# Layer 2 of a two-layer network by seven products: block sums of W2 kept in DRAM, and a fixed order of steps

## The chip, the cores and the metric

The kernel runs on one core of one Trainium2 chip. Its engines are TensorE (PE in the profile, its weight loads PEld), VectorE (DVE), ScalarE (ACT), GpSimd (POOL) and SyncE (SP), which issues most DMAs. The metric is the device time of one execution in microseconds (us).

## What is computed

```python
# q, k, v: (8, 8, 576, 64)
k_p = k.reshape(B, H, 72, 8, D).mean(axis=3)
v_p = v.reshape(B, H, 72, 8, D).mean(axis=3)
attn = softmax(q @ k_p.T / sqrt(D))            # 576 x 72 for each batch and head
x = (attn @ v_p) as (8, 576, 512)
xn = (x - mean(x)) / sqrt(var(x) + 1e-6) * g_ln
out = x + relu(xn @ w_ch1) @ w_ch2             # w_ch1: 512 x 2048, w_ch2: 2048 x 512
```

So there are 8 x 576 = 4608 tokens of 512 features. A small pooled attention makes x; then a network of two layers, the large part of the work, is added to it.

## The kernel before

**Chunks and tiles.** The tokens are cut into nine chunks of 512 (`CH`), each of four tiles of 128 (`TPC`). For a tile t, `stage_a` makes the attention scores and probabilities (`scores`, L495; `probs`, L523), and `stage_b` the values, the statistics of the normalisation and the normalised rows z (`values`, L612). For a chunk there is layer 1 (`ffn_in`, or from chunk 2 on `ffn_seven`) and layer 2 (`ffn_out`, L870).

**Precision by parts.** A product of two float32 matrices is made of float16 parts: each operand is a high part (rounded) plus a low part (the rest), and three matmuls, high x high, high x low and low x high, add up in PSUM. So each operand needs a pass that rounds (on ACT) and a pass that subtracts (on DVE or GpSimd). `split`, `parts_t` and `split_t` do this for weights, z and block sums.

**Seven products.** From chunk 2 on, layer 1 is made by Strassen's scheme in Winograd's form. Each operand is cut into 2 x 2 blocks, and seven block products take the place of eight. The right factors of W1 are the blocks B11, B21, B22 and the sums T1 to T4 (`sums_w`, `sum_last`, kept in SBUF), the left ones the blocks A11, A12, A22 of z and the sums S1 to S4, which `values` makes for the last two tiles of a chunk. `FACTOR` pairs them. `product` (L807) makes one of the seven for one block f of 128 hidden features: 6 matmuls of 128 x 128 weights on 256 columns. Products 1 and 6 and 7, 5 and 3, and 2 then 4 share a PSUM bank, so a bank is read out between two of them: `first_products`, `middle_products` and `last_product` copy the results out on ACT or add them on DVE, in a float32 buffer `cc`. Then, for each half of the tokens, ACT makes the ReLU's high part (L857) and DVE the low part (L858), into a `ring` tile.

**Layer 2** is made in the plain way: for a tile tt and a half of the hidden features, 24 matmuls of 512 columns (L882) add up in one PSUM bank, and one DVE instruction (L893) scales the sum by the token's factor and adds it to x. After the second half the rows are stored to `out`.

**Other work in the same queues.** GpSimd makes the pooled K and V of each of the eight batches (`pool_k` L368, `pool_v` L381) from loads on SP (`load_k`, `load_v`; two buffers each), the low part of the probabilities (L537) and those of z (L753). DMA transposes on SP turn probabilities and z (`transpose_z`, L756). `token_scales` (L712) makes 1/sqrt by three Newton steps on four numbers per partition, on DVE.

**Order.** Engines run their queues in program order. Chunks 0 and 1 and what belongs to them follow `START`, a list of steps written out by hand: a token such as `A.8` names a generator, here `stage_a(8)`, and each time it stands in the list the generator runs on to its next `yield`. From chunk 2 on a loop (L992) writes the order: per chunk 4 steps of `ffn_seven` and 4 of `ffn_out` for each half of the hidden features, with the next chunk's stages put between at the places `A_AT` and `B_AT`, and all the K and V work of a batch in one go.

**Memory.** PSUM has eight banks: two for scores and values (`ps_a`), six (`ps_g`) for the products. `ring` has two tiles for the hidden layer, `t_raw` two buffers for `cc`, `phl` two for the probabilities.

Of the kernel before, what the change touches and what calls it, by code (L numbers as in the profile page):

```python
# [104 lines left out]
def attn_ffn_kernel(ctx: ExitStack, tc: tile.TileContext, qT, kT, v, kvn, kvt, g, w1, w2, out):  # L105
# [506 lines left out]
    def values(t):  # L612
# [66 lines left out]
        if seven:  # L679
            yield  # L680
        (nc.gpsimd if c < 2 else nc.vector).tensor_scalar(
            out=z, in0=x, scalar1=ln[:, 0:1], scalar2=ln[:, 2:3], op0=ALU.subtract, op1=ALU.mult
        )
# [5 lines left out]
        elif tt < 2:  # L689
# [4 lines left out]
            yield from parts_t(z, 0, NKT, zTs[c][:, :, tt * P : (tt + 1) * P])  # L694
        else:
            zr, was = t_raw["z"], Z[t - 2]
            za = zr[:, 5 * HC : 7 * HC]
            nc.vector.tensor_scalar(
                out=za, in0=X[t - 2], scalar1=was[:, 0:1], scalar2=was[:, 2:3], op0=ALU.subtract, op1=ALU.mult
            )  # L700
# [104 lines left out]
    PS, C7 = {}, {}  # L805

    def product(c, h, f, m, start, stop):  # L807

        if start and m != 4:
            PS[f, m] = psum["ps_f"].tile([P, CH], F32, name="ps_f")  # L810
        ps = PS[f, {6: 1, 7: 1, 3: 5, 4: 2}.get(m, m)][:, :HC]
# [35 lines left out]
    def last_product(c, h, f):  # L847
        cc = C7.pop(f)
        u3 = product(c, h, f, 7, False, True)
        for j in range(2):  # L850
            nc.vector.tensor_tensor(out=cc[:, j, HC:], in0=u3, in1=cc[:, j, HC:], op=ALU.add)  # L851
# [188 lines left out]
```

## Time and profile before

| | us |
|---|---|
| median of three runs (lowest, highest) | 842.06 (841.86, 843.77) |
| the profiled execution | 842.33 |
| its span, first to last instruction | 840.6 |
| PE busy | 809.4 |
| DVE busy | 545.3 |
| POOL busy | 347.0 |
| ACT busy | 339.1 |

The profile is of one execution. Its span is what the instructions cover; the execution's own time is 1.7 us more. A line such as L882 is that line of the kernel. A group of instructions has one line, engine, operation and shape; it gives the count, the busy time (overlaps counted once), the mean length of one in ns, and the idle time of the engine ahead of them with what ended it. Matmuls overlap in the pipeline, so their mean length is more than their spacing. Of the span, the first 243 us hold the loading and splitting of the weights and chunks 0 and 1; chunks 2 to 8 fill the rest.

### The profile page before, as it was taken

The numbers are of one execution on the slowest core, as the hardware profiler recorded it, in microseconds if no ns is written. First come the engines' busy times: TensorE is split into PE (matmuls) and PEld (weight loads), VectorE is DVE, ScalarE is ACT, GpSimd is POOL, SyncE is SP. The second block draws the span as 40 slices with busy tenths as digits, with TensorE's granted clock in tenths as the row PEclk, the third lists the DMA queues.
The fourth block names the chain that finished last, engine by engine and source line by source line (L and its number), as shares of the span: only waits on it lengthen the run. The fifth ranks groups of instructions, "written<-read, shape, count | busy, mean of one in ns | idle before, by whom it ended". The sixth has DMA issues, their size and how long they took to land.

```text
span 840.6 us, 14847 instructions
## 1 busy us (share of the span) xinstructions
PE 809.4 (96%) x5742; PEld 527.5 (63%) x5742; DVE 545.3 (65%) x1110; ACT 339.1 (40%) x636; POOL 347.0 (41%) x497
## 2 busy tenths in 40 slices
PE   6797999999989999998999998999999999999998
PEld 3776454444557675757585857584858485858483
DVE  5988997674767476746764686559555856484242
ACT  4879784231424342423251515242524252424040
POOL 1898989684777442444225162402110211020000
PEclk9999999999999999999999999999999999999999
DMA  9848565232564515552434143513241424130001
GB/s 362 310 156 237 203 151 134 67 74 61 124 180 83 122 43 126 110 121 54 121 69 120 43 134 75 116 39 94 78 88 39 101 51 76 27 101 14 1 1 51
DMA packets 145975, 87.37 MB, mean 104 GB/s; under 512 B 125424, under 2 KB 126576, under 8 KB 143728
## 3 DMA queue, kind: packets, MB, share of 16 engines
q1 hardware_dynamic: 144752, 85.52, 39.2%
q10 hardware_dynamic: 1152, 0.90, 0.5%
q8 instruction: 45, 0.74, 0.4%
q14 instruction: 26, 0.21, 0.1%
HBM read 45.09 MB, written 9.44 MB: 65 GB/s over the span
## 4 chain that ended last, share of the span: by engine, by line
PE 70%; DVE 10%; POOL 9%; DMA 4%; issue 3%; ACT 2%; ACTq 0%; SPq 0%; POOLq 0%; DVEq 0%
PE ps_f L882 34%; PE ps_f L817 25%; PE ps_f L784 5%; PE ps_a L501 3%; DMA vr<-in_v_dram 2%; POOL vr L385 2%; POOL vr L386 1%; DVE w L264 1%; POOL vp L387 1%; POOL kblk L375 1%; PE ps_m L441 1%; POOL pt L575 1%; PE ps_a L633 1%; DVE w L211 1%; PE ps_a L634 1%
## 5 line engine op out<-in xcount | busy, mean ns | idle before, releaser
L882 PE MATMUL ps_f<-w,ring 128*128 128x512 f16 x1728 | 380.7, 379 | 0.0
L882 PEld LDWEIGHTS <-ring 128*128 128x128 f16 x1728 | 167.7, 98 | 193.8 <-issue 0.2
L817 PE MATMUL ps_f<-zts,w 128*128 128x256 f16 x1680 | 209.0, 274 | 8.2 <-DVE rowmax L168 3.4
L817 PEld LDWEIGHTS <-w 128*128 128x128 f16 x1680 | 164.2, 98 | 30.1 <-issue 8.9
L893 DVE SCALAR_TENSOR_TENSOR x<-ps_f,cy,x 128x512 f32<-128x512 f32 x72 | 53.8, 748 | 114.4 <-PE ps_f L882 107.8
L537 POOL TENSOR_TENSOR phl<-e,phl 128x512 f16<-128x512 f32 x32 | 38.5, 1204 | 142.5 <-ACT phl L527 142.4
L817 PE MATMUL ps_f<-zts,tsp 128*128 128x256 f16 x672 | 96.1, 272 | 0.3 <-ACT raw L835 0.3
L784 PE MATMUL ps_f<-zts,w 128*128 128x512 f16 (+1 forms) x480 | 87.0, 340 | 3.2 <-DVE ring L795 2.4
L857 ACT ACTIVATE ring<-raw 128x512 f16<-128x512 f32 x112 | 64.8, 622 | 58.4 <-DVE raw L851 57.9
L858 DVE SCALAR_TENSOR_TENSOR ring<-raw,ring 128x512 f16<-128x512 f32 x112 | 81.6, 755 | 8.7 <-ACT ring L857 8.4
L835 ACT COPY raw<-ps_f 128x256 f32<-128x256 f32 x56 | 20.8, 371 | 138.2 <-PE ps_f L817 134.8
L753 POOL TENSOR_TENSOR hl<-raw,hl 128x640 f16<-128x640 f32 x28 | 41.4, 1495 | 81.4 <-ACT hl L751 45.6
L784 PEld LDWEIGHTS <-w 128*128 128x128 f16 x480 | 47.0, 99 | 40.0 <-issue 3.7
L817 PEld LDWEIGHTS <-tsp 128*128 128x128 f16 x672 | 64.0, 98 | 10.7 <-issue 0.5
L385 POOL TENSOR_TENSOR vr<-vr 72x256 f32<-72x256 f32 x56 | 50.0, 898 | 34.3 <-DMA vr<-in_v_dram 34.0
L851 DVE TENSOR_TENSOR raw<-ps_f,raw 128x256 f32<-128x256 f32 x112 | 42.3, 418 | 22.6 <-PE ps_f L817 22.6
L838 DVE TENSOR_TENSOR raw<-ps_f,raw 128x256 f32<-128x256 f32 x56 | 23.7, 424 | 48.4 <-PE ps_f L817 43.0
L844 DVE TENSOR_TENSOR raw<-ps_f,raw 128x256 f32<-128x256 f32 x56 | 23.5, 420 | 32.6 <-PE ps_f L817 27.4
L751 ACT CAST hl<-raw 128x640 f16<-128x640 f32 x28 | 19.2, 722 | 62.6 <-DVE a L728 26.3
L501 PE MATMUL ps_a<-kblk,q 128*128 128x144 f32 (+1 forms) x320 | 43.1, 288 | 0.9 <-DVE st L661 0.9
L501 PEld LDWEIGHTS ps_a<-kblk,q 128*128 128x128 f32 (+1 forms) x320 | 39.1, 179 | 6.4 <-issue 1.3
L753 POOL TENSOR_TENSOR hl<-z,hl 128x512 f16<-128x512 f32 x18 | 21.5, 1196 | 36.0 <-ACT hl L751 22.7
(144 smaller groups left out, 1002.9 us busy)
## 6 DMA issues: line engine op xcount, KB each, us to landing
q<-in_qT_dram SPq DMA_DIRECT2D x36, 256.0 KB
out_dram<-x SPq DMA_DIRECT2D x36, 256.0 KB
tsp<-in_w_dram SPq DMA_DIRECT2D x8, 1024.0 KB
kr<-in_kT_dram SPq DMA_DIRECT2D x28, 288.0 KB
vr<-in_v_dram SPq DMA_DIRECT2D x56, 144.0 KB
raw<-in_w_dram SPq DMA_DIRECT2D x6, 1024.0 KB
ring<-in_w_dram SPq DMA_DIRECT2D x2, 1024.0 KB
w<-in_kT_dram SPq DMA_DIRECT2D x2, 576.0 KB
```

What stands on the lines that cost most here:

```text
L385: eng.tensor_add(out=vr[:, 0:4, :], in0=vr[:, 0:4, :], in1=vr[:, 4:8, :])
L501: nc.tensor.matmul(ps[r, p // 2, p % 2 * 2 * KV : (p % 2 + 1) * 2 * KV], lhsT=q[:, p, r], rhs=kblk[b % NKB][:, p, :], start=True, stop=True,)
L537: nc.gpsimd.tensor_tensor(out=ph[:, 0, :, KA:P], in0=e[:, :, 0:KA], in1=ph[:, 0, :, 0:KA], op=ALU.subtract)
L753: nc.gpsimd.tensor_tensor(out=zhl[:, 1, :], in0=src, in1=zhl[:, 0, :], op=ALU.subtract)
L784: nc.tensor.matmul(ps, lhsT=w[:, part, fs], rhs=zT[:, kz, cols], start=(n == 0), stop=(n == 3 * NKT - 1),)
L817: nc.tensor.matmul(ps, lhsT=w[:, part, f * P : (f + 1) * P], rhs=z, start=start and n == 0, stop=stop and n == 3 * KH - 1, skip_group_chec ...
L838: nc.vector.tensor_tensor(out=cc[:, 0, :HC], in0=m2, in1=cc[:, 0, :HC], op=ALU.add)
L851: nc.vector.tensor_tensor(out=cc[:, j, HC:], in0=u3, in1=cc[:, j, HC:], op=ALU.add)
L857: nc.scalar.activation(out=hh[:, 0, f], in_=cc[:, j], func=AF.Relu)
L858: nc.vector.scalar_tensor_tensor(out=hh[:, 1, f], in0=cc[:, j], scalar=0.0, in1=hh[:, 0, f], op0=ALU.max, op1=ALU.subtract)
L882: nc.tensor.matmul(ps, lhsT=h[:, part, i, cols], rhs=w[:, wp, j], start=(n == 0), stop=(n == 3 * NFT // 2 - 1),)
L893: nc.vector.scalar_tensor_tensor(out=x, in0=ps, scalar=out_scale(c, tt, half), in1=x, op0=ALU.mult, op1=ALU.add)
```

## The change

**Layer 2 of chunks 3 to 8 by seven products.** `out_seven(c, h, n, u)` makes product n of half h for 128 rows u: 12 matmuls on 256 columns, into three PSUM banks per u. After each product one DVE instruction scales what is in the bank and adds it to a 256-column half of x, or, for the last product, to both halves at once. `ffn_out` remains for chunks 0 to 2.

**The left factors** come from the hidden layer. `left_factors` makes the ReLU of the left half and splits A11 and A12, `right_relu` that of the right half and splits A22, `right_sums` makes S1 to S4 by four float32 sums of 256 elements on GpSimd, and `right_pair` splits them, two at a time: rounding on ACT, subtracting on DVE for S1 and S2, on GpSimd for S3 and S4. They lie where W2 was.

**The right factors** are W2's blocks and block sums. `keep_w2` stores B11, B21, B22 to a DRAM tile, `sums_w2` makes T1 to T4 (16 steps, during chunk 2 and the start of chunk 3) and stores them too. `load_w2` brings one factor of one half, 128 x 4096 bytes, back into one of four buffers in `ring`, 14 loads per chunk.

**Smaller edits.** From chunk 3 on z is normalised on ACT instead of DVE; product 7's two additions become one DVE instruction with the PSUM operand read twice; one of the two buffers of probabilities becomes the third `cc` buffer; `token_scales` is cut into steps. `first_products`, `middle_products`, `last_product` and `ffn_seven` are dissolved: each of the seven products and each later pass is a step of its own (`P`, `WH`, `EL`, `ER`, `ES`, `EP`, `O`, ...).

**A fixed order.** A list `STEADY` of 3398 tokens, built as `START` is, takes the place of the loop for chunks 2 to 8. All steps named above stand in it one by one, as do the single loads of W2, K and V and the single transposes.

```diff
+C_TWO = 3
-A_AT, B_AT = (0, 2, 5, 8), (4, 6, 11, 12)
+LO_GPSIMD = ()
+STEADY = """
+P.2.0.0.2 P.2.0.1.1 P.2.0.1.2 P.2.0.0.1 TW.0.0.0 TW.0.0.1 P.2.0.1.1 P.2.0.1.1 P.2.0.0.1 P.2.0.0.1 TW.0.0.0 TW.0.0.1
...
+O.5.1.1.1 O.5.1.1.1 O.5.1.0.0 O.5.1.0.0 O.5.1.1.0 O.5.1.1.0 B.27 B.27 ES.5.1.3 O.5.1.2.1 O.5.1.2.0 O.5.1.2.1 O.5.1.2.1
...
+O.8.1.5.1
+"""
...
-        ph = phl[t % 2]
+        ph = phl[t % 2 if t < 3 * TPC else 0]
...
+    def product(c, h, f, m):
+        if m in (1, 2, 5):
+            PS[c, h, f, m] = psum["ps_f"].tile([P, CH], F32, name="ps_f")
+        ps = PS[c, h, f, {6: 1, 7: 1, 3: 5, 4: 2}.get(m, m)][:, :HC]
...
+        yield
+        cc = left_buffer(c, h, f)
+        j, k = divmod({1: 0, 2: 0, 3: 2, 4: 1, 5: 3, 6: 2, 7: 1}[m], 2)
+        o = cc[:, j, k * HC : (k + 1) * HC]
+        if m in (2, 3):
+            nc.vector.tensor_tensor(out=o, in0=ps, in1=o, op=ALU.add)
+        elif m == 7:
+            o = cc[:, :, HC:]
+            nc.vector.tensor_tensor(out=o, in0=ps.unsqueeze(1).broadcast_to([P, 2, HC]), in1=o, op=ALU.add)
+        else:
+            nc.scalar.copy(out=o, in_=ps)
...
+    def split_h(src, n, f, engine):
+        hi, lo = (wt[2][:, n, a, f * HC : (f + 1) * HC] for a in range(2))
+        nc.scalar.copy(out=hi, in_=src)
+        yield
+        engine.tensor_tensor(out=lo, in0=src, in1=hi, op=ALU.subtract)
+
+    def left_factors(c, h, f):
+        cc = left_buffer(c, h, f)[:, :, :HC]
+        nc.scalar.activation(out=cc, in_=cc, func=AF.Relu)
+        yield from split_h(cc, slice(0, 2), f, nc.vector)
+
+    def right_relu(c, h, f):
+        cc = left_buffer(c, h, f)
+        nc.scalar.activation(out=cc[:, :, HC:], in_=cc[:, :, HC:], func=AF.Relu)
+        yield from split_h(cc[:, 1:2, HC:], slice(2, 3), f, nc.vector)
...
+    def right_sums(c, h, f):
...
+        nc.gpsimd.tensor_tensor(out=s_tmp[:, 0], in0=r01, in1=r11, op=ALU.add)
+        nc.gpsimd.tensor_tensor(out=s_tmp[:, 1], in0=s_tmp[:, 0], in1=r00, op=ALU.subtract)
+        yield
+        nc.gpsimd.tensor_tensor(out=s_tmp[:, 3], in0=r10, in1=s_tmp[:, 1], op=ALU.subtract)
+        nc.gpsimd.tensor_tensor(out=s_tmp[:, 2], in0=r00, in1=r01, op=ALU.subtract)
+
+    def right_pair(c, h, f, i):
+        yield from split_h(s_tmp[:, 2 * i : 2 * i + 2], slice(3 + 2 * i, 5 + 2 * i), f, nc.gpsimd if i or c in LO_GPSIMD else nc.vector)
...
+    def sums_w2(h, f, e):
...
+        for i in range(2):
...
+            nc.vector.tensor_tensor(
+                out=b[:, 2 * i : 2 * i + 2], in0=src[:, 0, e::2], in1=src[:, 1, e::2], op=ALU.add
+            )
+        yield
+        b11, b12, b21, b22 = (b[:, i] for i in range(4))
+        nc.gpsimd.tensor_tensor(out=b11, in0=b12, in1=b11, op=ALU.subtract)
+        nc.gpsimd.tensor_tensor(out=b12, in0=b22, in1=b12, op=ALU.subtract)
+        yield
+        nc.gpsimd.tensor_tensor(out=b22, in0=b22, in1=b11, op=ALU.subtract)
+        nc.gpsimd.tensor_tensor(out=b21, in0=b21, in1=b22, op=ALU.subtract)
+        yield
+        nc.scalar.copy(out=t[:, :, 0], in_=b)
+        yield
+        nc.gpsimd.tensor_tensor(out=t[:, :, 1], in0=b, in1=t[:, :, 0], op=ALU.subtract)
...
+    W2_USE = (("A11", "B11"), ("A12", "B21"), ("A22", "T4"), ("S1", "T1"), ("S2", "T2"), ("S4", "B22"), ("S3", "T3"))
...
+    def load_w2(c, h, n):
+        nc.sync.dma_start(out=w2_buffer(c, h, n), in_=w2s[h][W2_AT[W2_USE[n][1]]])
...
+    def out_seven(c, h, n, u):
+        left, b = H_AT[W2_USE[n][0]], w2_buffer(c, h, n)
+        if n in (0, 1, 3):
+            PO[c, h, u, n] = psum["ps_f"].tile([P, CH], F32, name="ps_f")
+        ps = PO[c, h, u, {0: 0, 1: 1, 2: 1, 3: 3, 4: 0, 5: 3, 6: 0}[n]][:, :HC]
+        for f in range(FPQ):
+            for part, wp in ((0, 0), (0, 1), (1, 0)):
+                nc.tensor.matmul(
...
+        yield
...
+        nc.vector.scalar_tensor_tensor(out=x, in0=ps, scalar=scale, in1=x, op0=ALU.mult, op1=ALU.add)
...
-    for c in range(2, NRUN):
...
-            all_of(op(*args))
+    run(STEADY)
```

More of the change, by code (lines that the diff above doesn't have):

```diff
@@ L802, in ffn_in, with left_buffer @@
         )
[L805 to L811, printed above, removed]
+    PS, C_BUF = {}, []
+    def left_buffer(c, h, f):
+        if "c" not in t_raw:
+            t_raw["c"] = t_raw.pop("t1").rearrange("p n c -> p (n c)").rearrange(
+                "p (i f c) -> p i f c", i=2, f=2
+            )
+        if c < C_TWO:
+            return t_raw["c"][:, f % 2]
+        if not C_BUF:
+            raw = phl[1].rearrange("p a h k -> p (a h k)").bitcast(F32).rearrange("p (i c) -> p i c", c=CH)
+            C_BUF.extend((t_raw["c"][:, 0], t_raw["c"][:, 1], raw))
+        return C_BUF[(2 * FPQ * c + FPQ * h + f) % 3]
+    def product(c, h, f, m):
+        if m in (1, 2, 5):
+            PS[c, h, f, m] = psum["ps_f"].tile([P, CH], F32, name="ps_f")
+        ps = PS[c, h, f, {6: 1, 7: 1, 3: 5, 4: 2}.get(m, m)][:, :HC]
         lname, rname = FACTOR[m]
@@ new lines, in attn_ffn_kernel @@
+    PO = {}
+    def out_seven(c, h, n, u):
[6 more added lines that the diff above has]
+                nc.tensor.matmul(
+                    ps,
+                    lhsT=wt[2][:, left, part, f * HC + u * P : f * HC + (u + 1) * P],
+                    rhs=b[:, f // FPB, wp, f % FPB],
+                    start=n < 4 and f == 0 and part == wp == 0,
+                    stop=f == FPQ - 1 and part == 1,
+                    skip_group_check=True,
+                )
+        yield
+        tt = u + 2 * (n in (2, 3, 6))
+        t = c * TPC + tt
+        x, scale = X[t], out_scale(c, tt, h)
+        if n == 6:
+            x = x.rearrange("p (j c) -> p j c", j=2)
+            ps = ps.unsqueeze(1).broadcast_to([P, 2, HC])
+        else:
+            x = x[:, HC:] if n in (3, 4, 5) else x[:, :HC]
+        nc.vector.scalar_tensor_tensor(out=x, in0=ps, scalar=scale, in1=x, op0=ALU.mult, op1=ALU.add)
+        if h == 1 and n in (5, 6):
+            yield
+            nc.sync.dma_start(out=out[t * P : (t + 1) * P, :], in_=X.pop(t))
@@ L975, in all_of, with run @@
             pass
-    begun = {}
-    with tc.manual_schedule():
-        for token in START.split():
-            if token not in begun:
-                name, *args = token.split(".")
-                begun[token] = iter(ops[name](*map(int, args)) or ())
-            next(begun[token], None)
-        for steps in begun.values():
-            all_of(steps)
+    def run(tokens):
+        begun = {}
+        with tc.manual_schedule():
+            for token in tokens.split():
+                if token not in begun:
+                    name, *args = token.split(".")
+                    begun[token] = iter(ops[name](*map(int, args)) or ())
+                next(begun[token], None)
+            for steps in begun.values():
+                all_of(steps)
+    run(START)
     first.close()
```

412 lines of the change are left out of this document (345 added, 67 removed).

## The prediction

> **What bounds the kernel now.** I read the page first for the share of each engine, then the busy times of the seven seven-product chunks side by side, then the chain that ended last for the pace of a matmul, and last what TensorE waited for.
>
> ```profile
> span 840.6 us, 14847 instructions
> ...
> PE 809.4 (96%) x5742; PEld 527.5 (63%) x5742; DVE 545.3 (65%) x1110; ACT 339.1 (40%) x636; POOL 347.0 (41%) x497
> ```
>
> The whole run is TensorE's. By chunk, from the first product of chunk 2 (columns: start and end, length, busy time of PE, PEld, DVE, ACT, POOL, granted clock, DMA share, GB/s):
>
> ```profile
> 243.00:331.00 88.00, 85.82 (x633) 57.87 (x632) 54.13 (x123) 30.16 (x64) 44.33 (x79) 0.98 0.44 105
> 331.00:418.00 87.00, 84.37 (x628) 57.86 (x627) 54.78 (x122) 31.44 (x67) 36.43 (x60) 1.00 0.44 99
> 418.00:503.50 85.50, 85.50 (x652) 58.07 (x650) 55.83 (x118) 31.59 (x67) 31.89 (x51) 1.00 0.37 93
> 503.50:590.40 86.90, 84.58 (x627) 57.79 (x625) 56.13 (x123) 31.17 (x67) 23.34 (x37) 1.00 0.37 84
> 590.40:675.50 85.10, 85.10 (x651) 58.04 (x650) 52.34 (x113) 30.70 (x66) 15.39 (x18) 1.00 0.32 72
> 675.50:758.60 83.10, 83.10 (x618) 56.74 (x617) 51.56 (x111) 30.67 (x66) 13.95 (x14) 1.00 0.33 64
> 758.60:840.60 82.00, 78.28 (x529) 51.56 (x527) 29.58 (x57) 20.24 (x48) 0.00 (x0) 1.00 0.05 17
> ```
>
> TensorE idles 2.18, 2.63 and 2.32 us in chunks 2, 3 and 5, together 7.1 us, and 3.72 us at the end, where the last row block is scaled and stored. Nothing else has more than two thirds of a chunk. So in these 597.6 us time falls only if TensorE gets less to do, and rises if another engine gets more than TensorE has.
>
> **The pace of a matmul.** The groups by shape mislead here:
>
> ```profile
> L882 PE MATMUL ps_f<-w,ring 128*128 128x512 f16 x1728 | 380.7, 379 | 0.0
> L817 PE MATMUL ps_f<-zts,w 128*128 128x256 f16 x1680 | 209.0, 274 | 8.2 <-DVE rowmax L168 3.4 <-DVE x L893 1.8 <-DVE raw L838 1.5
> L817 PE MATMUL ps_f<-zts,tsp 128*128 128x256 f16 x672 | 96.1, 272 | 0.3 <-ACT raw L835 0.3
> ```
>
> Busy time over count gives 380.7/1728 = 220 ns for 512 columns and (209.0+96.1)/2352 = 130 ns for 256. But these groups alternate in short runs, and the pipeline's tail is counted at the end of each run. In the chain (start, length, what) a long run stands undisturbed:
>
> ```profile
> 132.69 15.54 PE ps_f L882 x72
> ...
> 758.76 16.38 PE ps_f L817 x150
> ```
>
> 15.54/72 = 215.8 ns for 512 columns, 16.38/150 = 109.2 ns for 256, each with its own weight load. Halving a matmul costs 1%, not 18%.
>
> **What goes, on TensorE.** Layer 2 of a chunk is 192 matmuls of 512 columns, 41.4 us. By seven products it is 2 halves x 7 products x 2 row blocks x 12 = 336 of 256 columns, 36.7 us. That is 4.74 us less per chunk, 28.5 us in six. Scores, values and layer 1 keep their matmuls. The profiled run took 842.33 us, 1.7 us more than its span and 0.3 us more than the median: 842.33 - 28.5 = 813.8 us if all idle time stays, 806.7 us if the 7.1 us go too. Busy time also counts the tail of the matmul ahead of a gap, 379 - 216 = 0.16 us by the rows above, so some idle time is hidden in it; for about 20 ends of runs I allow 3 us, and 803 us is the floor.
>
> The idle time, by what ended it:
>
> ```profile
> PE ps_f L817 <- DVE rowmax L168: 3.4, 2, 2.6
> PE ps_f L817 <- DVE x L893: 1.8, 2, 1.3
> PE ps_f L817 <- DVE raw L838: 1.5, 1, 1.5
> ```
>
> The 3.4 us are the maximum over V, whose small matmul stands in TensorE's order ahead of products that don't need it. The fixed order can put it, and the products that need late transposes, behind others, so I let these gaps go and charge what is new.
>
> **What comes, on DVE and ACT.** I build chunk 6 from its row (52.34 and 30.70 us) and these:
>
> ```profile
> L858 DVE SCALAR_TENSOR_TENSOR ring<-raw,ring 128x512 f16<-128x512 f32 x112 | 81.6, 755 | 8.7 <-ACT ring L857 8.4
> L857 ACT ACTIVATE ring<-raw 128x512 f16<-128x512 f32 x112 | 64.8, 622 | 58.4 <-DVE raw L851 57.9
> L893 DVE SCALAR_TENSOR_TENSOR x<-ps_f,cy,x 128x512 f32<-128x512 f32 x72 | 53.8, 748 | 114.4 <-PE ps_f L882 107.8
> L851 DVE TENSOR_TENSOR raw<-ps_f,raw 128x256 f32<-128x256 f32 x112 | 42.3, 418 | 22.6 <-PE ps_f L817 22.6
> ```
>
> DVE loses, per chunk, 16 of L858 (12.1 us) and the 8 evictions L893 (6.0), and its 16 adds L851 (6.7) become 8 of 512 elements (6.0). It gains 8 x (two low parts of 512 and one of 256) = 8 x 1.93 = 15.4, and 28 evictions of layer 2, 24 of 256 and 4 of 512, 13.0 us. That makes 62 us of about 80, less what the six normalisations moved to ACT give back. ACT loses 16 of L857 (10.0) and gains five passes of 512 and one of 256 (no dearer than 0.62) per block, 8 x 3.7 = 29.9, and six normalisations, 3.7: 54 us of 80. Both fit. What lies behind a late DVE instruction is an eviction, and behind that a product that adds onto the same bank (the first and the fifth, the second and the third). Two products of 1.3 us lie between most such pairs and an eviction takes 0.42, so I price this at 2.5 us, bounds 0 and 9 (a whole L893, 0.75 us, in each of the 12 halves). In chunk 2 the sums over W2 add 32 DVE passes of 256 (13.4 us on 54.1) and 16 ACT passes (10.0 on 30.2), which the 84 us there cover. The probabilities share one buffer from chunk 3 on; their tiles are some 20 us apart, so I cost that at nothing.
>
> **What comes, on GpSimd.** This is where the change can fail. Its prices, from chunk 2 on:
>
> ```profile
> L753 POOL TENSOR_TENSOR hl<-raw,hl 128x640 f16<-128x640 f32 x24 | 35.4, 1492 | 75.3 <-ACT hl L751 39.5 <-issue 35.9
> L537 POOL TENSOR_TENSOR phl<-e,phl 128x512 f16<-128x512 f32 x23 | 26.6, 1156 | 141.0 <-ACT phl L527 141.0
> L385 POOL TENSOR_TENSOR vr<-vr 72x256 f32<-72x256 f32 x29 | 23.3, 810 | 31.4 <-DMA vr<-in_v_dram 31.3
> L753 POOL TENSOR_TENSOR hl<-z,hl 128x512 f16<-128x512 f32 x12 | 14.6, 1218 | 28.0 <-ACT hl L751 14.8 <-DVE raw L698 8.5 <-issue 3.7
> L386 POOL TENSOR_TENSOR vr<-vr 72x128 f32<-72x128 f32 x30 | 13.9, 471 | 0.5
> L375 POOL TENSOR_TENSOR kblk<-kr 64x72 f32<-64x72 f32 x32 | 13.7, 427 | 4.0 <-PE ps_a L501 2.5
> L371 POOL TENSOR_TENSOR kr<-kr 128x288 f32<-128x288 f32 x14 | 11.5, 821 | 23.9 <-DMA kr<-in_kT_dram 23.8
> L387 POOL TENSOR_TENSOR vp<-vr 72x64 f32<-72x64 f32 x30 | 9.6, 330 | 4.5 <-DVE vb L211 2.5 <-DVE cvm L640 1.4
> L372 POOL TENSOR_TENSOR kr<-kr 128x144 f32<-128x144 f32 x14 | 7.2, 521 | 0.2
> L540 POOL TENSOR_TENSOR phl<-e,phl 128x64 f16<-128x64 f32 x23 | 7.0, 305 | 0.0
> L673 POOL COPY ln<-cv 128x2 f32<-128x2 f32 x18 | 5.6, 347 | 3.7 <-DVE cv L461 3.5
> ```
>
> Four sums of 256 elements go by L385 (0.81), a low part of 512 by L537 (1.16), W2's four sums of 128 by L386 (0.47). I count the fixed order from its start to the first V step of the last batch, well into chunk 4's last products. TensorE has there 170 products of layer 1 (111.3 us), the 8 row blocks of chunk 2 (41.4), 48 products of layer 2 (62.9) and 13 tiles of scores and 12 of values, some 1.5 us together for each (chunk 6's 85.1 less its 78.1 us of products, over five tiles), 19 us: 235 us. GpSimd has 64 sums (51.8), 16 low parts (18.5), all 16 W2 sums at 4 x 0.47 + 1.16 (48.6), 12 pairs of K at 0.82 + 0.52 + 2 x 0.43 (26.4), 31 heads of V at 0.81 + 0.47 + 0.33 (49.9), 13 probability splits (15.0), 12 z parts of 640 and 6 of 512 (25.2), 13 tails L540 and 12 copies L673 (8.1): 243 us, 8 more than TensorE. GpSimd, half idle so far, thus gets as much as TensorE for nearly three chunks, in a queue where each instruction waits for the one before. After that batch it falls to 51 us of 80: 15.39 + 8 x (4 x 0.81 + 1.16).
>
> These rows hold the collisions of today, and the change adds more. A DVE instruction with two SBUF inputs and a GpSimd one exclude each other (start, length, instruction):
>
> ```profile
> 319.78 0.15 DVE L729 TENSOR_TENSOR a<-a,ve 128x4 f32<-128x4 f32 x1
> 320.34 2.76 POOL L753 TENSOR_TENSOR hl<-raw,hl 128x640 f16<-128x640 f32 x2 [4.22 <-ACT hl L751]
> 320.36 1.40 DVE L729 TENSOR_TENSOR a<-a,ve 128x4 f32<-128x4 f32 x1
> ```
>
> The same four-element product took 0.15 us alone and 1.40 us when GpSimd had begun 0.02 us before: it waited for that whole instruction. The stretch has about 48 such DVE passes of 512 elements and 72 of 256; if each stopped GpSimd for half its 755 or 418 ns, that is 33 us; if none did more than today's, nothing. The Trainium skill, "SBUF — State Buffer", section "SBUF: two separate sides", calls it an exclusive lock held for a whole instruction and speaks against this change, which puts work on both sides of it; the trace agrees (1.40 against 0.15). By that rule, with every pass colliding, the sum would come to the top of the third case below.
>
> I take 9 us for GpSimd: the 8 of the sum and little of the collisions, since K and V may be late for a while and only S1 to S4 hold TensorE up. Bounds: 0, and the 41 of sum and collisions.
>
> **What moves, on the queues.** SP gains 14 loads of 0.5 MB per chunk, 7.3 MB in 80 us, about 92 GB/s on the 72 of chunk 6, with 38 stores in chunk 2, those of the second half's sums the last, a whole half before their use; a load waits until the product four places back is done, and K, V, Q loads and transposes stand behind it. Four products of two blocks last 10.5 us, so the loads are covered at four buffers; uncovered, the price is in the last case.
>
> Sum: 806.7 + 9 + 2.5 = 818 us.
>
> **The rivals.** *The order holds:* GpSimd's idle stretches in the order take up the excess, 803 to 808 us. For it: the rows' means hold waits, L385's 0.81 us and L753's 1.49 among them, so the bare instructions take less; against it: a GpSimd that is busy all the time meets DVE more often, not less. *GpSimd sets the pace:* the collisions are paid, 806.7 + 8 + half to all of 33 = 831 to 848 us; for it the 1.40 us row; against it, that a pass only collides when GpSimd is busy, and that L858 has a mean of 755 ns today beside a half-busy GpSimd. *Slower:* GpSimd's queue waits for K and V loads. Place: chunks 2 to 4, where an instruction that adds K or V rows stands ahead of the sums for S1 to S4 and its load has not landed. Price: the idle times in the rows L385 and L371, 31.3 + 23.8 = 55 us for the same loads, free so far since GpSimd was half idle. All of it on top of the 8 gives 870 us; it decides from 30 of the 55 on, since then GpSimd is 38 us late and 806.7 + 38 = 844.9 is the first time that counts as slower. Against it: the order puts each load well ahead of its use. *Not what it says:* 256-column products at 130 ns would make layer 2 43.7 us and gain nothing; the long run excludes it.
>
> **Chances.** Forecast, 808 to 831 us: 0.55. The order holds: 0.15. GpSimd sets the pace: 0.20. Loads hold GpSimd: 0.10. A measurement of this kernel can tell about 0.3% from no change, so faster means under 839.8 us: 0.55 + 0.15 + 0.13 of the third case = 0.83. Its part from there to 844.9 us has 0.05. Its top, 0.02, and the last case make slower 0.12. The range from the floor of 803 to 842 us leaves out those and half of the middle part.
>
> **What would show it.** In the changed profile: from chunk 3 on no matmul of 512 columns and 672 of 256 at 109.2 ns per chunk; POOL at nine tenths or more from 243 to about 480 us and some six tenths after; TensorE's new waits there behind the low parts of S1 to S4, at the fourth to seventh product of a half; the last two chunks without gaps, about 78 and 77 us. Wrong if the pace of 256 columns exceeds 112 ns, if the idle time lies in the last chunks, or if it ends on DVE's evictions or on W2's loads.

## The result and the profile after

The changed kernel takes 835.88 us (median of six runs, 834.55 to 839.23) beside 842.74 us of the kernel before on the same chip: a ratio of 0.9929, 95% interval 0.9902 to 0.9955. It is faster by 6.9 us. The forecast was 818 us: the direction was right and the range held, but the gain is little more than a quarter of the 24 us forecast.

Line numbers from here on are those of the changed kernel: L1134 the matmuls of `product`, L1251 those of `out_seven`, L1268 its VectorE eviction, L1170 the ScalarE cast and L1172 the subtraction that make a high and a low part (`split_h`; the subtraction is on VectorE or on GpSimd), L1189 to L1193 GpSimd's sums for S1 to S4, L1021 to L1023 the Newton steps behind the tokens' inverse roots, L1213 the first adds of W2's block sums. L1148 adds a product from PSUM to `cc` on VectorE, L1153 copies one on ScalarE, L1059 makes z's low parts on GpSimd, L1164 the low parts of the plain hidden layer, L1285 has the matmuls of the plain layer 2, and L442 the maximum over V. The page:

```profile
span 833.7 us, 17487 instructions
...
PE 787.5 (94%) x6606; PEld 609.8 (73%) x6606; DVE 671.7 (81%) x1242; ACT 472.5 (57%) x880; POOL 615.3 (74%) x817
```

DVE rose from 65% to 81% and POOL from 41% to 74%, while PE fell from 96% to 94%: TensorE got less to do and waits more. The steady part in stretches (start and end, length, busy time of PE, PEld, DVE, ACT, POOL, granted clock, DMA share, GB/s):

```profile
243.00:331.00 88.00, 82.25 (x645) 56.20 (x644) 79.57 (x142) 43.30 (x87) 76.79 (x122) 1.00 0.63 151
331.00:411.00 80.00, 76.59 (x683) 64.09 (x681) 68.69 (x130) 51.20 (x103) 76.20 (x107) 0.99 0.74 200
411.00:491.00 80.00, 76.81 (x750) 67.60 (x748) 71.19 (x133) 50.38 (x102) 68.43 (x94) 0.99 0.67 182
491.00:571.00 80.00, 76.87 (x736) 68.14 (x733) 67.35 (x132) 48.09 (x98) 60.39 (x84) 1.00 0.70 185
571.00:651.00 80.00, 76.80 (x756) 68.04 (x757) 68.34 (x128) 48.81 (x100) 55.40 (x72) 1.00 0.64 170
651.00:731.00 80.00, 78.08 (x756) 70.02 (x754) 65.16 (x130) 51.04 (x103) 48.63 (x56) 1.00 0.56 154
```

The idle time is in every stretch, also where POOL has fallen to 49 us of 80. DVE stands at 65 to 71 us of 80 throughout. What TensorE waits for (total, times, longest):

```profile
PE ps_f L1251 <- DVE w L1172: 7.2, 8, 1.7
PE ps_f L1251 <- DVE x L1268: 7.1, 8, 1.5
PE ps_f L464 <- DVE rowmax L442: 2.9, 1, 2.9
PE ps_f L1285 <- DVE ring L1164: 2.1, 4, 1.0
PE ps_f L1251 <- DVE phl L1148: 0.6, 1, 0.6
...
PE ps_f L1251 <- POOL w L1172: 0.2, 1, 0.2
```

All of the first five end on VectorE: on its low parts, on its evictions, on the maximum over V. On the low parts that GpSimd makes, TensorE waits only 0.2 us.

To compare runs I use two sums over each trace. *Idle time*: from the first product of the steady part on, what the distance between the starts of two matmuls exceeds the median of its kind by, where that is over 0.02 us; this also counts the gaps that busy time hides. *Waits* of an engine: what each of its instructions after 243 us took beyond the quickest twentieth of its kind. By the first, the 6.9 us of span come apart so: TensorE's own work after the first product (each matmul at the median of its kind) falls from 582.3 to 555.4 us, that product starts 2.2 us earlier, the idle time rises from 12.3 to 34.0 us, and the tail is 0.3 us longer; -26.9 - 2.2 + 21.7 + 0.3 = -7.1, which is the 6.9 within what the small distances leave out. The forecast had about 17 us of idle time. The second sum says where to look: VectorE's waits rose from 32 to 110 us, GpSimd's from 14 to 47, ScalarE's are 5. Some groups of VectorE (count, busy us, mean ns):

```profile
L1172 DVE TENSOR_TENSOR w<-raw,w 128x256 f16<-128x256 f32 x32 | 23.9, 749 | 2.2 <-ACT w L1170 2.2
L1213 DVE TENSOR_TENSOR kr<-w 128x256 f32<-128x256 f16 x28 | 22.1, 829 | 0.7 <-POOL phl L1226 0.4
L1022 DVE TENSOR_TENSOR a<-a,ve 128x4 f32<-128x4 f32 x21 | 11.6, 553 | 0.7
L1268 DVE SCALAR_TENSOR_TENSOR x<-ps_f,y,x 128x256 f32<-128x256 f32 x72 | 33.0, 475 | 18.0 <-PE ps_f L1251 17.8
L1148 DVE TENSOR_TENSOR raw<-ps_f,raw 128x256 f32<-128x256 f32 x80 | 32.6, 414 | 18.7 <-ACT raw L1153 9.5 <-PE ps_f L1134 8.6 <-ACT phl L1153 0.4
```

The quickest twentieth of these groups is at 410, 412 and 161 ns for the first three. The last two, which read one operand from PSUM (`ps_f`), are hardly stretched. One place, start and length:

```profile
406.75 0.72 POOL L1192 TENSOR_TENSOR w<-raw,w 128x256 f32<-128x256 f32 x1
406.92 2.19 DVE L1172 TENSOR_TENSOR w<-raw,w 128x256 f16<-128x256 f32 x1
407.43 0.72 POOL L1193 TENSOR_TENSOR w<-raw 128x256 f32<-128x256 f32 x1
408.11 0.72 POOL L1189 TENSOR_TENSOR w<-raw 128x256 f32<-128x256 f32 x1
...
409.17 0.28 PE L1251 MATMUL ps_f<-ring,w 128*128 128x256 f16 x1 [1.68 <-DVE w L1172]
```

A low part of 0.41 us took 2.19: it began 0.17 us behind a GpSimd sum and came out after the third. TensorE, which needed it, stood 1.68 us.

### The profile page after: what moved, and what is told of

Same layout as the page of the kernel before. It is cut to its first block, busy times and chain, and to the rows that moved or that the text cites. A ratio compares the mean times of both kernels' runs of the same rounds, so it can differ in the third digit from the quotient of the medians.

```text
span 833.7 us, 17487 instructions
## 1 busy us (share of the span) xinstructions
PE 787.5 (94%) x6606; PEld 609.8 (73%) x6606; DVE 671.7 (81%) x1242; ACT 472.5 (57%) x880; POOL 615.3 (74%) x817
## 4 chain that ended last, share of the span: by engine, by line
PE 58%; DVE 25%; POOL 9%; DMA 3%; issue 3%; ACT 2%; ACTq 0%; SPq 0%; POOLq 0%; DVEq 0%
PE ps_f L1134 20%; PE ps_f L1251 15%; PE ps_f L1285 10%; PE ps_f L1090 7%; DVE w L1172 4%; DVE x L1268 2%; DVE w L537 2%; PE ps_a L774 2%; DVE w L484 1%; DVE a L1022 1%; POOL w L1172 1%; DMA vr<-in_v_dram 1%; DMA pt<-phl 1%; DVE x L924 1%; DMA raw<-in_w_dram 1%
## 5 line engine op out<-in xcount | busy, mean ns | idle before, releaser
L1251 PE MATMUL ps_f<-ring,w 128*128 128x256 f16 x2016 | 235.3, 274 | 15.7 <-DVE w L1172 7.2
L1251 PEld LDWEIGHTS <-w 128*128 128x128 f16 x2016 | 196.3, 98 | 45.0 <-issue 10.7
L1134 PE MATMUL ps_f<-zts,w 128*128 128x256 f16 x1680 | 206.3, 273 | 1.5 <-DVE x L1296 0.8
L1134 PEld LDWEIGHTS <-w 128*128 128x128 f16 x1680 | 163.4, 98 | 21.9 <-issue 2.7
L1285 PE MATMUL ps_f<-w,ring 128*128 128x512 f16 x576 | 127.2, 379 | 2.1 <-DVE ring L1164 2.1
L1153 ACT COPY raw<-ps_f 128x256 f32<-128x256 f32 x160 | 56.8, 372 | 103.0 <-PE ps_f L1134 94.0
L1285 PEld LDWEIGHTS <-ring 128*128 128x128 f16 x576 | 55.6, 98 | 69.5 <-DVE ring L1164 5.1
L1134 PE MATMUL ps_f<-zts,tsp 128*128 128x256 f16 x672 | 91.2, 273 | 0.3 <-DVE raw L1148 0.2
L1170 ACT CAST w<-w 128x512 f16<-128x512 f32 x96 | 58.9, 618 | 50.1 <-POOL w L1190 25.4
L1090 PEld LDWEIGHTS <-w 128*128 128x128 f16 x480 | 47.3, 100 | 40.1 <-issue 3.7
L1172 POOL TENSOR_TENSOR w<-w 128x512 f16<-128x512 f32 x48 | 58.2, 1213 | 20.1 <-ACT w L1170 16.5
L1134 PEld LDWEIGHTS <-tsp 128*128 128x128 f16 x672 | 65.3, 98 | 8.8 <-issue 1.0
L1268 DVE SCALAR_TENSOR_TENSOR x<-ps_f,y,x 128x256 f32<-128x256 f32 (+1 forms) x84 | 41.6, 515 | 25.6 <-PE ps_f L1251 25.1
L1189 POOL TENSOR_TENSOR w<-raw 128x256 f32<-128x256 f32 x32 | 24.1, 752 | 49.1 <-ACT raw L1181 31.3
L1172 DVE TENSOR_TENSOR w<-raw,w 128x512 f16<-128x512 f32 (+1 forms) x64 | 53.3, 839 | 2.9 <-ACT w L1170 2.9
L1059 POOL TENSOR_TENSOR hl<-raw,hl 128x640 f16<-128x640 f32 x28 | 41.7, 1499 | 14.3 <-ACT hl L1057 12.2
L658 POOL TENSOR_TENSOR vr<-vr 72x256 f32<-72x256 f32 x56 | 51.3, 915 | 0.5
L1268 DVE SCALAR_TENSOR_TENSOR x<-ps_f,cy,x 128x256 f32<-128x256 f32 (+1 forms) x84 | 42.0, 516 | 11.8 <-PE ps_f L1251 11.1
L1148 DVE TENSOR_TENSOR raw<-ps_f,raw 128x256 f32<-128x256 f32 x80 | 32.6, 414 | 18.7 <-ACT raw L1153 9.5
L1172 DVE TENSOR_TENSOR w<-w 128x512 f16<-128x512 f32 x48 | 40.4, 841 | 7.4 <-ACT w L1170 7.3
```

What stands on the lines that cost most here:

```text
L658: eng.tensor_add(out=vr[:, 0:4, :], in0=vr[:, 0:4, :], in1=vr[:, 4:8, :])
L1059: nc.gpsimd.tensor_tensor(out=zhl[:, 1, :], in0=src, in1=zhl[:, 0, :], op=ALU.subtract)
L1090: nc.tensor.matmul(ps, lhsT=w[:, part, fs], rhs=zT[:, kz, cols], start=(n == 0), stop=(n == 3 * NKT - 1),)
L1134: nc.tensor.matmul(ps, lhsT=w[:, part, f * P : (f + 1) * P], rhs=z, start=m in (1, 2, 4, 5) and n == 0, stop=m in (2, 3, 4, 7) and n == 3 ...
L1148: nc.vector.tensor_tensor(out=o, in0=ps, in1=o, op=ALU.add)
L1153: nc.scalar.copy(out=o, in_=ps)
```

## The experiments

Three theories went into them. **A**: VectorE's passes with two SBUF inputs wait for GpSimd's reading instructions, VectorE gets late, and TensorE with it. **B**: the fixed order and VectorE's own, undisturbed load make the idle time. **C**: GpSimd's queue is too long and the right factors are late. Times are medians; the ratio is to the kernel before on the same chip (841.2 to 844.1 us, from one group of runs to the next), and for the changed kernel it is 0.9929. Two times from different groups can be some 3 us apart for that reason alone, so a difference of that size between two rows is not sure.

| kernel | us | ratio, 95% interval | idle us | VectorE's waits us |
|---|---|---|---|---|
| before | 842.74 | 1 | 12.3 | 32 |
| changed | 835.88 | 0.9902 to 0.9955 | 34.0 | 110 |
| sums_no_read | 836.37 | 0.9908 to 0.9952 | 32.9 | 77 |
| pool_no_read | 848.04 | 1.0042 to 1.0085 | 46.2 | 8 |
| newton_pool | 853.74 | 1.0091 to 1.0171 | no profile | no profile |
| order_only | 853.24 | 1.0096 to 1.0186 | 24.1 | 23 |
| pool_light | 806.75 | 0.9537 to 0.9619 | 3.5 | 8 |
| fill_early | 841.16 | 0.9966 to 1.0024 | 42.0 | 105 |
| s34_dve | 845.20 | 1.0016 to 1.0062 | 45.2 | 103 |
| dve_light | 818.35 | 0.9669 to 0.9756 | 14.4 | 97 |
| pool_matched | 806.33 | 0.9513 to 0.9605 | 4.9 | 8 |
| dve_fill | 852.65 | 1.0071 to 1.0161 | 51.3 | 119 |
| lo_late | 866.72 | 1.0230 to 1.0305 | 61.8 | 110 |
| tw_light | 829.64 | 0.9790 to 0.9873 | 26.5 | 85 |
| matched_fill | 814.94 | 0.9630 to 0.9687 | 12.7 | 9 |
| sums_matched | 824.83 | 0.9735 to 0.9803 | 23.6 | 75 |
| newton_none | 828.82 | 0.9794 to 0.9853 | 27.7 | 94 |
| few_passes | 831.50 | 0.9816 to 0.9871 | 29.2 | 103 |
| few_signed | 831.75 | 0.9835 to 0.9890 | 31.3 | 103 |

### First runs: less reading, a longer queue, the order alone

**sums_no_read.** The four sums of `right_sums` read one column and fill the rest (written out here for the first of them):

```diff
-nc.gpsimd.tensor_tensor(out=s_tmp[:, 0], in0=r01, in1=r11, op=ALU.add)
+nc.gpsimd.tensor_tensor(out=s_tmp[:, 0, 0:1], in0=r01[:, 0:1], in1=r11[:, 0:1], op=ALU.add)
+for _ in range(2):
+    nc.gpsimd.memset(s_tmp[:, 0], 0.5)
```

> GpSimd's four sums per block (S1 to S4, chunks 3 to 8) are replaced by a sum of one column and two fills of the same tile, so GpSimd is as long busy and waits for the same data, but hardly reads SBUF. Layer 2 of those chunks thus gets constant sums. Theory A (port): DVE's passes with two SBUF inputs wait for GpSimd's reading instructions, DVE's evictions and low parts come late, and TensorE idles behind them. Then DVE's time over its bare durations (110 us after 243 us, 32 before the change) falls by about a third to 75, TensorE's idle time from 34 us to some 24, the time to about 826. Rival B (tight order): the idle comes from bank after bank in a DVE that is busy for 81% by its own work. Rival C (GpSimd's queue): the factors come late because GpSimd is full. B and C: no change, 833 to 838.

Measured 836.37 us: VectorE's waits fell to 77 us, as A said, and the time did not fall, against A. But a one-column sum took 0.20 to 0.32 us in the means of its groups, and 384 more instructions made GpSimd's queue 30 us longer (its instructions and the gaps under 0.13 us between them, from 243 to 830 us: 487 us, beside 457 in the changed kernel). Two things had changed at once; sums_matched below mends it.

**pool_no_read.** The same for GpSimd's other large passes in the steady part too (low parts, z parts, the first two sums of K and V, score lows, W2's sums).

> As the run before, and also the W2 sums, the low parts made on GpSimd (of probabilities, z, S3 and S4) and the first two sums of each K and V pooling, from chunk 2's order on, are replaced by a one-column operation and fills of equal time. Low parts are zero, sums constant, K and V partly pooled. A: DVE's time over its bare durations falls under 25 us, TensorE's idle time to 14 us or less, the time to about 815. B and C: idle time stays near 34 us and the time at 832 to 838.

Measured 848.04 us: VectorE's waits are gone (8 us) and the kernel is slower. GpSimd's queue had grown to 512 us:

```profile
243.00:331.00 88.00, 79.99 (x616) 56.04 (x615) 55.10 (x132) 41.10 (x84) 74.99 (x279) 0.96 0.58 140
331.00:411.00 80.00, 70.06 (x600) 55.42 (x598) 48.48 (x118) 43.41 (x91) 69.89 (x252) 0.98 0.67 177
...
651.00:731.00 80.00, 79.44 (x780) 71.28 (x778) 59.23 (x137) 51.34 (x105) 53.20 (x166) 1.00 0.62 159
```

With the gaps between 252 instructions GpSimd is full from 331 to 411 us, and TensorE loses 10 us there; from 651 us on GpSimd has room, and TensorE is all but busy. So C's mechanism is real for a queue this long, and A's gain shows where it is not.

**newton_pool.** The Newton steps go to GpSimd from the fourth chunk on (there in four instructions a step instead of three).

> The Newton steps of the tokens' scales (two-input instructions on four numbers, 0.37 to 0.55 us on DVE against 0.16 bare) go from DVE to GpSimd from chunk 3 on; nothing is left out. A: DVE loses 18 us of waiting, idle falls by 3 to 6 us, 830 to 833. B: DVE loses its 7 to 25 us of busy time, idle falls by 1 to 2 us, 834. C: GpSimd gets some 16 us more in a full queue, slower, 838 to 845.

Measured 852.1 to 854.3 us in three runs; the profiled execution took 4651.56 us and is left out. Adding to GpSimd's queue cost about 18 us, more than C had said, and VectorE's relief did not show. This spoke for C.

**order_only.** The fixed order with the plain layer 2 (`ffn_out`) in the last six chunks and without W2's sums; I placed the row blocks in the list myself.

> The fixed order alone: the same list without the steps of the seven products of layer 2 and of W2's block sums; the row blocks of the plain layer 2 and the ReLU steps stand in their places. TensorE's own work is back at that of before. If the order by itself makes the idle time (B), idle is 20 us or more and the time 850. A: GpSimd is down to the load it had before, idle is 8 us or less against 12 before, the time 836 to 841. C: the same as A.

Measured 853.24 us. The list, with my places for layer 2, costs some 10 us over the kernel before, while GpSimd is busy only 172 us after 243 us. It is another list than the changed kernel's, so it can't say what that one costs; pool_matched does.

### Second runs: each engine made light

**pool_light.** All those GpSimd passes on one column, without the fills (but for the tiles that nothing else writes).

> From the start of the fourth chunk on, GpSimd's large passes over S1 to S4 and their low parts, over the z parts' low halves, the keys' and values' first two sums and the scores' lows are made on one column only (the rest of those tiles stands as it was or is filled), so these parts of the computation are left out. GpSimd then has neither a full queue nor long reads. Both A (VectorE held by GpSimd's reads) and C (GpSimd's queue too long in chunks 3 to 5) expect TensorE's idle time after 241 us to fall from 34 to about 12 us, as before the change: about 815 us. B (the fixed order and VectorE's own load make the idle time, GpSimd aside) expects 25 us of idle or more: 827 to 836 us. Where the idle time goes from tells A and C apart: C expects the first 240 us of the steady part to gain most, A expects the last chunks to gain too.

Measured 806.75 us with 3.5 us of idle time. The order of the changed kernel has no cost of its own, and VectorE's own work fits it. B falls. Most of the gain lies in TensorE's first 240 us of work (22.1 us of idle time in the changed kernel, 2.6 here), as C said, but the last 235 gained too (6.5 and 0.9), as A said.

**fill_early.**

```diff
+if c < 6:
+    nc.gpsimd.memset(s_tmp[:, 0], 0.5)
 nc.gpsimd.tensor_tensor(out=s_tmp[:, 0], in0=r01, in1=r11, op=ALU.add)
```

and the same ahead of the third sum.

> In chunks 3 to 5 each step of the S sums gets one more GpSimd instruction ahead of it, a fill of 256 elements that reads no SBUF: 48 fills of 0.31 us and the gap behind each, about 18 us more of GpSimd's queue and no more reading. C expects most of it in the time: 846 to 854 us. A and B expect no change: 835 to 838 us.

Measured 841.16 us, 5 us more for 15 us of queue (472 beside 457), between the two. The length of the queue costs, but about half of the least that C said.

**s34_dve.**

```diff
-nc.gpsimd if i or c in LO_GPSIMD else nc.vector
+nc.gpsimd if i and c > 5 else nc.vector
```

> In chunks 3 to 5 the low parts of S3 and S4 go from GpSimd to VectorE: GpSimd loses 24 passes of 1.15 us, 27.6 us, VectorE gets 24 of 0.68 us bare, 16.3 us, 5.4 us in each chunk. The result is the same. C expects 826 to 831 us, since GpSimd's queue is what is full there. A and B expect no gain or a loss, since VectorE is busy 69 to 71 us of 80 there: 836 to 844 us.

Measured 845.20 us, 9 us more with 27.6 us less for GpSimd. C's remedy makes it worse. The longest stall, 5.2 us, begins so:

```profile
504.99 0.72 POOL L1193 TENSOR_TENSOR w<-raw 128x256 f32<-128x256 f32 x1
505.67 1.39 POOL L1059 TENSOR_TENSOR hl<-raw,hl 128x640 f16<-128x640 f32 x1
505.74 0.62 ACT L1170 CAST w<-w 128x512 f16<-128x512 f32 x1 [0.97 <-POOL w L1193]
506.39 2.77 DVE L1172 TENSOR_TENSOR w<-w 128x512 f16<-128x512 f32 x2 [2.23 <-ACT w L1170]
```

The moved low part made VectorE wait 2.23 us for a cast that waited for GpSimd's sum, and then the two low parts were held by GpSimd's next pass: 2.77 us for two passes of 0.68.

**dve_light.** VectorE's low parts on one column (`lo[..., 0:1]` and so on).

> The low parts that VectorE makes in the last six chunks (of the relu'd blocks and of S1 and S2) are made on one column only; the rest of them is left out. VectorE loses 144 passes, about 70 us by their bare times, 12 us a chunk, and more by their measured ones; GpSimd's instructions stay. B (VectorE's load under the fixed order) expects TensorE's idle time to fall by half or more: 815 to 820 us. C expects little in chunks 3 to 5, where GpSimd sets the pace, and some in the last: 829 to 836 us. A lies between, since fewer passes of VectorE are held: 822 to 830 us.

Measured 818.35 us. GpSimd's instructions are all there and read as before; VectorE's busy time from 243 to 833 us fell by 72 us (485 to 413) and the time by 17.5. From 331 us on 5.8 us of idle time are left. This is inside B's range, 4 us below A's and 11 below C's, so A missed it. Since pool_light leaves B no room by itself, the reading is that VectorE is late by its own work and its waits together: 17.5 us for 72 us of VectorE's time here, and in later runs 7 for 28 (newton_none), 11 for 35 (sums_matched) and 21 for 101 (matched_fill), a fifth to a third of each microsecond.

### Third runs: reading and queue taken apart

**pool_matched.** As pool_no_read, with fills cut so that a pass takes as long as the one that it replaces:

```diff
+nc.gpsimd.tensor_tensor(out=out[..., 0:1], in0=in0[..., 0:1], in1=in1[..., 0:1], op=op)
+nc.gpsimd.memset(dst, value)
+if times == 2:
+    nc.gpsimd.memset(dst[..., : dst.shape[-1] // 2], value)
```

> GpSimd's large passes from the fourth chunk's steps on are put in another form: one column of the pass and then fills, which read no SBUF, so that each takes about as long as the pass that it replaces (0.83 us for the 256-element sum, 1.16 for the 512-element low part); that arithmetic is left out. GpSimd's queue is as long as in the changed kernel, its reading is gone. A (VectorE held by GpSimd's reads) expects VectorE at some 57 us of 80 and TensorE's idle time after 241 us at 5 to 15 us: 807 to 818 us. C (GpSimd's queue) expects no gain: 833 to 845 us.

Measured 806.33 us:

```profile
331.00:411.00 80.00, 79.58 (x759) 71.39 (x757) 58.57 (x138) 52.09 (x106) 67.89 (x249) 1.00 0.78 203
...
571.00:651.00 80.00, 80.00 (x803) 71.79 (x802) 58.68 (x136) 52.28 (x105) 48.04 (x167) 1.00 0.71 181
```

GpSimd's queue is 435 us and TensorE idles 4.9 us in all. VectorE has gone from 68 to 58.6 us in these stretches with the same passes. Its groups (L1193, L1040, L1288 are the former L1172, L1022, L1268):

```profile
L1193 DVE TENSOR_TENSOR w<-raw,w 128x256 f16<-128x256 f32 x32 | 13.4, 422 | 3.5 <-ACT w L1188 3.5
L1040 DVE TENSOR_TENSOR a<-a,ve 128x4 f32<-128x4 f32 x21 | 3.5, 166 | 0.7
L1288 DVE SCALAR_TENSOR_TENSOR x<-ps_f,y,x 128x256 f32<-128x256 f32 x72 | 33.9, 481 | 31.8 <-PE ps_f L1271 31.4
```

749 ns became 422 and 553 became 166; the eviction from PSUM kept its 475 to 481.

**dve_fill.** VectorE's low parts become one column and two fills.

> VectorE's 144 low parts of the last six chunks are replaced by one column and two fills that read no SBUF and take about their bare time, 0.68 us for 512 and 0.41 for 256 elements; that arithmetic is left out. VectorE's bare load is unchanged; a third of its reading passes is gone. A expects its waits of 110 us to fall to about 75 and the idle time of 34 us by a third to a half: 819 to 826 us. A theory of VectorE's bare load under the fixed order expects no change: 833 to 837 us.

Measured 852.65 us, and the run can't part A from its rival. VectorE's waits hardly fell, since the one-column passes were held as the full ones had been: the 144 of them waited 34.2 us, the full ones 34.6. (The sum of 119 us is too high by some 20: behind the fills the quickest evictions took 362 ns in place of 469, so that the others seem to wait.) And the fills brought a wait that the changed kernel has not, ScalarE's next cast behind VectorE's fill:

```profile
ACT w L1170 <- DVE w L1175: 8.0, 7, 3.0
```

It shows that the waits go by the number of passes and not by their length.

**lo_late.**

```diff
-LO_GPSIMD = ()
+LO_GPSIMD = (6, 7, 8)
```

> In the last three chunks the low parts of S1 and S2 go from VectorE to GpSimd (the switch that the kernel has): VectorE loses 24 passes of 0.93 us as measured, 7.4 us a chunk, GpSimd gets 24 of 1.2 us, 9.6 us a chunk, where it is busy 49 to 60 us of 80. The result is the same. A expects half of the 9 us of idle time of these chunks to go, less what the added reading takes back: 830 to 835 us. C expects a loss or nothing: 835 to 842 us.

Measured 866.72 us, 31 more than the changed kernel: all theories missed. GpSimd is no fuller than 56 us of 80 there (from 571 us on), but its queue is in order:

```profile
676.10 0.73 POOL L1193 TENSOR_TENSOR w<-raw 128x256 f32<-128x256 f32 x1
676.78 1.40 POOL L1059 TENSOR_TENSOR hl<-raw,hl 128x640 f16<-128x640 f32 x1
678.13 2.27 POOL L1172 TENSOR_TENSOR w<-w 128x512 f16<-128x512 f32 x2
679.35 0.39 PE L1251 MATMUL ps_f<-ring,w 128*128 128x256 f16 x1 [5.15 <-POOL w L1172]
```

The low part that TensorE waits for stands behind a sum and a z part. The row `PE ps_f L1251 <- POOL w L1172` holds 21.2 us in seven such waits, and 0.2 us in the changed kernel. A step moved between engines is moved behind another queue.

**tw_light.** W2's block sums on one column, behind one fill; the sums are left out.

> The 16 steps that make W2's block sums in the third chunk work on one column, behind one fill that reads nothing; the sums are left out, their loads, stores and ScalarE copies stay. This prices the sums on VectorE and GpSimd: of the 8.5 us of idle time in the first 80 us of TensorE's steady work, all theories expect 4 to 7 us to go if VectorE's and GpSimd's work there is what is late (829 to 832 us), and none if it is the scores' maxima and the ring of layer 2's left factors that this stretch waits for anyway (835 to 837 us).

Measured 829.64 us, 6.2 less: the sums over W2, made once in the third chunk, cost that on VectorE and GpSimd. The forecast had given them nothing on VectorE.

### Last runs

**matched_fill.** pool_matched with the fills of fill_early. GpSimd's queue is then 452 us, beside 457 in the changed kernel.

> The kernel whose large GpSimd passes read one column only (that arithmetic is left out), with the 48 further fills of chunks 3 to 5 ahead of the S sums: about 18 us more of GpSimd's queue, which is then as long as in the changed kernel as it runs (some 455 us between 243 and 830 us), and reads nothing. A (VectorE held by GpSimd's reads) expects 806 to 814 us. C (the length of GpSimd's queue) expects two thirds or more of the changed kernel's loss to be back: 824 to 838 us.

Measured 814.94 us, 1 us above A's range and 9 below C's. With a queue as long as the changed kernel's, and hardly any reading, 21 us are gone.

**sums_matched.** The sums of S1 to S4 alone, by one column, one fill and a fill of a quarter.

> Only the S sums' 192 passes read one column and fill the rest (that arithmetic is left out), with fills cut so that each pass takes about 0.77 us, no longer than the sum that it replaces (0.72 us alone, 0.82 as run). In the earlier form each had taken about 0.9 us, and GpSimd's queue had grown by 30 us. A expects VectorE's waits at 75 instead of 110 us and 5 to 12 us less time: 824 to 831 us. C expects the time of the changed kernel: 833 to 838 us.

Measured 824.83 us, waits 75 us, both as A said; the queue is 457 us, as in the changed kernel. Of sums_no_read's missing gain, GpSimd's longer queue was the cause: the two differ in the second fill alone.

**newton_none.** `if c > 1: continue` in the loop of three steps in `token_scales`.

> The three Newton steps behind each chunk's inverse root are left out from the third chunk on: 63 VectorE passes of 4 elements, 28.4 us as measured, of which 18.5 us are waits. GpSimd stays. A expects the idle time to fall as it did per us of VectorE's time when the low parts were left out (18 us for 72): 826 to 831 us. C, and a theory that such short passes hide in VectorE's idle time, expect 834 to 837 us.

Measured 828.82 us, as A said: 7 less for 63 passes of four elements, with GpSimd's instructions kept.

**few_passes and few_signed.** From this a version with the whole computation:

```diff
-for _ in range(3):
+for _ in range(3 if c < 2 else 2):
...
-nc.vector.scalar_tensor_tensor(
-    out=ln[:, 0:1], in0=ln[:, 0:1], scalar=-1.0, in1=ln[:, 2:3], op0=ALU.mult, op1=ALU.mult
-)
+nc.scalar.activation(out=ln[:, 2:4], in_=cv[:, 1:3], func=AF.Identity)
+nc.scalar.activation(out=ln[:, 0:1], in_=ln[:, 0:1], func=AF.Identity, scale=ln[:, 2:3])
+nc.scalar.activation(out=ln[:, 0:1], in_=ln[:, 0:1], func=AF.Identity, scale=-1.0)
```

The copy of the two constants, which GpSimd made, goes to ScalarE too. Each Newton step turns the sign of its result, so few_passes, with one step fewer, leaves out one turn; few_signed turns it back in the product that follows.

> The changed kernel with fewer small passes on VectorE: two Newton steps in place of three from the third chunk on (21 passes, about 9.5 us as measured, less precise by that step), and in the last six chunks the product of mean and scale, 24 passes of one column, 11 us as measured, as two ScalarE instructions; the copy of two constants goes from GpSimd to ScalarE too. VectorE loses some 20 us. By the rate of the runs before (18 us for 72, 7 for 28) A expects 5 us: 829 to 833 us. Theories without VectorE's waits expect 834 to 837 us.

> As few_passes, with the sign that the left-out Newton step would have turned put into the product behind it, which costs no instruction: the result of the changed kernel, but for the rounding of one Newton step. The time of few_passes again: A expects 829 to 834 us, theories without VectorE's waits 834 to 837 us.

Measured 831.50 and 831.75 us. few_signed has the ratio 0.9862 (0.9835 to 0.9890) to the kernel before, beside 0.9902 to 0.9955 of the changed kernel: it is faster than both, if not by much. GpSimd's 24 copies went as well, so not all of the 4 us need be VectorE's.

## Why the prediction was right or wrong

**TensorE's part was right.** Long runs after the change keep the forecast pace (start, length, what; 109.2 ns each):

```profile
757.44 21.61 PE ps_f L1134 x198
811.15 18.35 PE ps_f L1251 x168
```

TensorE's work fell by 26.9 us after the first product, and that product starts 2.2 us earlier: 29.1 us beside the 28.5 forecast. The case in which the order holds (803 to 808) was where this leads if nothing else is late: pool_light and pool_matched stand at 806.75 and 806.33 us, the forecast's 806.7 with all old idle time gone. In the changed kernel not all of it went: the maximum over V still holds TensorE 2.9 us.

**GpSimd's 9 us came out near in size, in part by luck.** With the changed kernel's queue and hardly any reading, matched_fill is 8.6 us over pool_matched. But the forecast got its 8 us by adding up passes at 0.81 us a sum and the like. In pool_matched a sum with its fills took about that (0.83 us in the median), the queue was 435 us, and nothing was lost. The 8.6 us came with the 17 us of queue on top; in the changed kernel GpSimd's own waits (47 us, beside 26 in pool_matched) make it that long. Nor did TensorE wait where the forecast put it, behind the low parts of S1 to S4: of the 7.2 us behind VectorE's low parts 1.0 are S1's and S2's, with 0.2 behind GpSimd's S3 and S4; the rest are those of A11, A12 and A22, which need nothing of GpSimd. The queue is full where the forecast had it (76.79 of 88, 76.20 and 68.43 of 80 us busy up to 491 us; with the gaps 82, 80 and 72), and falls to three quarters and then six tenths after. On top of those 435 us each further microsecond of queue cost about half of one: 8.6 us for 17 here, 42 for the 77 of pool_no_read. The rival of the K and V loads did not come: GpSimd waited 0.5 us for K's, and nothing waits for W2's.

**VectorE's 2.5 us were the step that failed.** "Both fit. What lies behind a late DVE instruction is an eviction, [...] so I price this at 2.5 us, bounds 0 and 9." The load fits: bare, as in pool_matched, VectorE is busy 56 to 60 us of 80 from 331 us on, beside 62 forecast (ScalarE 48 to 51, beside 54). But the forecast's 62 were made of the means before the change, with the waits of a half-idle GpSimd in them, and in the changed kernel VectorE stands at 65 to 71: a low part of 512 elements, put at 755 ns, took 841 to 928. The waits that the change adds to VectorE were priced nowhere. The forecast quoted the row that shows them, a four-element pass of 1.40 us in place of 0.15, and then charged the collision to the other side only: so many VectorE passes that stop GpSimd, 33 us at most, little of it taken. GpSimd's waits did grow by 33 us (14 to 47), but VectorE's by 78 (32 to 110), and it is VectorE's that reach TensorE. Against matched_fill, which has the queue and hardly any of the reading, the changed kernel is 20.9 us longer (22.8 by the ratios): that is the term that stood as 2.5, with 9 as its upper bound. The split is made in this order, queue first; the two act together, as sums_no_read showed, and another order would share them out otherwise. 806.3 + 8.6 + 20.9 = 835.8.

The Trainium skill, "SBUF — State Buffer", section "SBUF: two separate sides", says that a VectorE instruction with two SBUF inputs and a GpSimd instruction that reads SBUF exclude each other: whichever starts first holds a shared pair of ports, as an exclusive lock, for its whole length. The traces agree on both conditions: beside GpSimd's fills the low part of 256 elements took 422 ns, beside its sums 749, and the evictions with a PSUM input took nearly the same in both (475 and 481).

**The case "GpSimd sets the pace"** gave 831 to 848 us, and the time lies in it, but not for its reason: taking GpSimd's low parts away made the kernel slower (s34_dve), and leaving VectorE's out, with GpSimd's instructions kept, made it 17.5 us faster.

**What was to show it wrong** did so in part: there is idle time in the last chunks (6.5 us in TensorE's last 235 us of work), though most of the 34.0 us lies earlier, and 7.1 us of waits end on VectorE's evictions.

## What to carry to other kernels

Where VectorE and GpSimd both get work on SBUF, add VectorE's two-input passes at their price beside a GpSimd as busy as it will be (here 749 for 410 ns at 256 elements, 553 for 161 at 4), not at their bare one or that of today, and on both engines. The wait went by the number of passes here, so small ones on VectorE are the first to leave out or to give to ScalarE, and a pass that read one operand from PSUM was not held. Before moving a step to the emptier engine, look at what stands ahead of it in that engine's queue and what it will itself hold up there.

## What was not expected of the hardware

A VectorE pass that is held can miss its turn between GpSimd's instructions: the 0.41 us pass above waited through three sums in a row, 2.19 us. A GpSimd sum of one column still took about 0.2 us where 256 columns took 0.72, so cutting GpSimd's work into more instructions made its queue longer, not shorter (487 us beside 457). And the engine that lost most by the collisions was not the one with the longer instructions: GpSimd's sums of 720 ns were stretched to 750 to 930 ns, VectorE's passes of 410 ns to 710 to 830.
